# The product e(e+2) of Mish: from VectorE to GpSimd for four of the first five hidden tiles of a block

## The chip, the cores and the metric

The kernel runs on one core of a Trainium2 chip. A core has five engines, each of which works through a queue of its own in order: TensorE (PE in the profile; its weight loads are PEld), VectorE (DVE), ScalarE (ACT), GpSimd (POOL) and SyncE (SP, which issues the DMAs). Semaphores order them. The metric is the device time of one execution in microseconds (us).

## The reference

One transformer block with modulated layer norms, float32, one sequence of 2048 tokens, width 512, 32 heads of 16, hidden width 1792:

```
sa, ca, ga, sb, cb, gb = split(silu(c) @ w_mod)
h = layernorm(x) * (1 + ca) + sa
x = x + ga * (softmax(q k^T / 4) v @ wo)          # q, k, v = h @ wqkv
h = layernorm(x) * (1 + cb) + sb
x = x + gb * (mish(h @ w1 + b1) @ w2)             # mish(z) = z * tanh(log(1 + exp(z)))
```

With e = exp(z), tanh(log(1 + e)) = e(e+2) / (e(e+2) + 2). The kernel works with that form: u = e(e+2), r = exp(-log(u + 2)), one Newton step on r, and z * u * r.

## The kernel before

**Steps.** Attention is cut into 4 blocks of 512 queries (NB) and 8 groups of 4 heads (G), and each pair of these into 16 chunks of 128 keys, so that there are T = 512 steps t. A step makes four score products (`score`, L529, 128 keys by 512 queries), whose exponential ScalarE writes as `pr` (L532), and four products of 128 queries by 512 keys for the row maxima of a later group (`max_tile`, L480), which VectorE reduces to `mx` (L482). At its end stand the products of the exponentials with v, for the step two before (`pv`, L547). Scores and maxima go through one PSUM ring of 6 banks (`ring`): TensorE can write a bank only after ScalarE or VectorE has read the product that was in it.

**Half steps.** Time in the program is counted in half steps h = 2t and 2t + 1. `at(h, f)` puts a piece of work into the list of half step h. In `step`, `run_hooks(2 * t)` issues the first list ahead of the step's products, and `run_hooks(2 * t + 1)` issues the second in the midst of the products, at `i == len(mine) // 2`. An early-listed piece thus stands in its engine's queue ahead of the four exponentials or maxima of its step, and one of an odd half step stands between them: where a step's part of a unit has six slots, after the first exponential and after the second maximum.

**Units beside the attention.** The output projection and the dense layers of a query block that is done run beside the attention of the next ones. Their work is cut into units of 12 matmuls (24 of half the width in a block's first up unit), fed from a list, half of them in each pair of steps; one unit takes four steps. `block(qb, t0)` makes the list for each of the first three query blocks; the fourth is done by `tail()` after the last step. An up unit `up_unit(f)` computes hidden tile f, 128 of the 1792 hidden values (f = 0 to 13) for 512 tokens. The list begins with up units 0, 1, 2, 3, 4 one right after the other (so every 8 half steps one ends); then down units (back to width 512, `down_unit`) and up units take turns, so that an up unit ends every 16 half steps.

**Mish.** When an up unit's last matmul is issued, its `fin(h)` runs: it issues stage s1 and lists the other stages of `mish` at h plus a lag:

- s1 (L737, ScalarE): hb = product + bias, frees the PSUM bank `bk` that the next unit writes
- s2 (L740, ScalarE): ee = relu(10 - hb), with which e is capped
- s2b (L743, ScalarE): ee = exp(10 - ee), which is e
- s3 (L747 or L749 and L750): ee = e(e+2), on VectorE as one instruction if `own`, otherwise on GpSimd as two; then on GpSimd hb = hb * ee (L751) and qq = ee + 2 (L753)
- s4 (L756, ScalarE): rr = log(ee + 2)
- s5 (L759, ScalarE): rr = exp(-rr), then six instructions on GpSimd (L765 to L768, then `hi_copy` L95 and `lo_sub` L98), which leave the hidden tile as the pair a_h, a_l that the down units read

For f = 0, 1, 2 the lags are 2, 4, 5, 6, 8, so s5 falls together with s1 of the next up unit. For f = 3, whose result the first down units wait for, they are 1, 2, 3, 4, 6. For f = 4 and above they are taken from the free even half steps, s3 half a step after s2b, and s4 in the next even one, mostly 2, 4, 5, 6 and a later one for s5. `idle(h)` is true for half steps late in the third block's time, where no maxima are left and VectorE has room.

The profile's execution shows 42 such up units; 17 have the product on VectorE (5 in each of the three blocks, and 2 in idle half steps), 25 on GpSimd. The 14 hidden tiles of the tail have it on VectorE.

Of the kernel before, what the change touches and what calls it, by code (L numbers as in the profile page):

```python
# [18 lines left out]
def adaln_block(ctx: ExitStack, tc: tile.TileContext, x, wqkv, wo, w1, b1, w2, c, w_mod, out):  # L19
# [142 lines left out]
    def bank(tag="ms"):  # L162
        return ring() if tag == "ring" else ps.tile([P, TB], F32, tag=tag, name="bk", bufs=1)
# [38 lines left out]
    def at(h, f):  # L202

        hooks.setdefault(h, []).append(f)
# [508 lines left out]
    def up_mms(acc, w, hh, hl, parts=1):  # L713
        for c in range(parts):
            s = slice(c * TB // parts, (c + 1) * TB // parts)
            mm3(acc[:, s], [w1v(w, 0, k) for k in range(DK)], [w1v(w, 1, k) for k in range(DK)],
                [hh[:, k, s] for k in range(DK)], [hl[:, k, s] for k in range(DK)], "b")
# [58 lines left out]
    def idle(h):  # L776

        return h is not None and 2 * (T - PRO) + 2 < h <= 2 * T
# [6 lines left out]
    def block(qb, t0):  # L785
# [7 lines left out]
        def load(h, d, load_, keys):  # L793

            for j, k in enumerate(keys):
                at(h + 2 * j, lambda k=k: d.__setitem__(k, load_(k)))
# [76 lines left out]
        def up_unit(f, tag):  # L873
            mst["norming"] = False
            w = w1s.pop(f)
            acc = bank(tag)
            up_mms(acc, w, *hx, parts=1 if f else 2)
            stages = mish(f, acc, False, act)

            def fin(h):  # L880
                stages[0](idle(h))
                own = f < 5 or idle(h + 5)
                if f < 4:
                    lags = (1, 2, 3, 4, 6) if f == 3 else (2, 4, 5, 6, 8)
                else:

                    free = [i for i in range(2, 16, 2) if i != 8 and (h + i) % 32 != 4]
                    lags = (free[0], free[1], free[1] + 1, free[2], free[3])
                for i, s in zip(lags, stages[1:]):
                    at(h + i, (lambda s=s: s(True)) if i == lags[2] and own else s)  # L890
                done["a", f] = h + lags[-1]
                nxt = state[qb + (f + 2) // FT][1] if f + 2 < FT or qb < NB - 2 else None
                if nxt is None:
                    if f == FT - 1:
                        load(h + 1, state[last][1], w1_tail, (2, 3))
                else:
                    load(h, nxt, load_w1, ((f + 2) % FT,))
            return fin
# [58 lines left out]
        for gi in range(2):  # L957
            f = 4 * gi + 5
# [526 lines left out]
```

## Time and profile before

| | |
|---|---|
| median of 3 runs | 1699.01 us (1698.46 to 1699.34) |
| profiled execution, its own time | 1697.49 us |
| its span | 1695.7 us |
| TensorE busy | 99% |
| VectorE / ScalarE / GpSimd busy | 85% / 80% / 48% |
| mean granted TensorE clock | 0.999 of full speed |

How to read it: the span is that of the instructions in the trace, and the execution's own time has some 1.8 us more around it. The rows of the order of time show the start in us from the span's start, the duration, the engine, the line in the code, the operation, output and inputs, the count of merged instructions, and in brackets how long the engine sat idle before and what ended that. Neighbouring instructions on VectorE and ScalarE overlap a little, so that four exponentials of about 0.6 us each take 2.06 us. The rows with L547 mark the end of a step: the time from one to the next is the length of a step.

### The profile page before, as it was taken

To read this page: it belongs to the slowest core of one execution; us is meant where nothing else is said; L and a number is where in the kernel's file an instruction comes from. 1 tells how busy PE (TensorE), PEld (TensorE's weight loads), DVE (VectorE), ACT (ScalarE), POOL (GpSimd) and SP (SyncE) were. 2 spreads that over 40 slices of the span, in tenths; PEclk is the share of its full clock that TensorE was granted. 3 is DMA by queue.
4 is the path that set the end of the run, shared out by engine and by line. 5 is a ranking of instruction groups with operands and counts; after the bars stand their busy time and mean duration, and the time that the engine had idled before them with its cause. 6 is when DMAs were issued, how large, how long until landed. Compare 5 with 4: busy or idle time off the path is not lost.

```text
span 1695.7 us, 33728 instructions
## 1 busy us (share of the span) xinstructions
PE 1672.8 (99%) x12406; PEld 924.7 (55%) x12406; DVE 1437.8 (85%) x2370; ACT 1358.3 (80%) x2612; POOL 820.1 (48%) x838
## 2 busy tenths in 40 slices
PE   7999999999999999999999999999999999999999
PEld 5755665555445455555555455555555455555587
DVE  6888888888899888888889898888889988884378
ACT  6247777777778988888888998888888988888674
POOL 6456223665413464655423564555323564555442
PEclk9999999999999999999999999999999999999999
DMA  6887546777755342534355434434354433433261
GB/s 234 237 274 193 135 127 185 232 218 212 229 170 140 100 107 75 136 80 126 81 155 148 117 74 98 134 72 134 84 142 128 130 93 77 143 107 128 77 230 62
DMA packets 114029, 238.44 MB, mean 141 GB/s; under 512 B 23824, under 2 KB 49424, under 8 KB 107912
## 3 DMA queue, kind: packets, MB, share of 16 engines
q1 hardware_dynamic: 113864, 236.28, 49.3%
q8 instruction: 98, 1.61, 0.4%
q14 instruction: 67, 0.55, 0.1%
HBM read 179.95 MB, written 51.44 MB: 136 GB/s over the span
## 4 chain that ended last, share of the span: by engine, by line
PE 91%; DVE 4%; ACT 2%; DMA 2%; issue 0%; SPq 0%; POOL 0%; ACTq 0%; DVEq 0%
PE bk L547 29%; PE ring L529 23%; PE ring L480 20%; PE bk L136 9%; PE bk L129 3%; PE ring L1156 2%; DVE mx L482 2%; PE ring L129 2%; ACT pr L532 1%; DMA xt<-in_A_x 1%; PE ring L494 1%; DMA qa<-mt 1%; PE ring L859 0%; PE ring L509 0%; DVE hf L392 0%
## 5 line engine op out<-in xcount | busy, mean ns | idle before, releaser
L482 DVE TENSOR_REDUCE mx<-ring 128x1 f32<-128x512 f32 x1968 | 1223.0, 682 | 153.1 <-PE ring L480 137.4
L532 ACT ACTIVATE pr<-ring 128x512 f32<-128x512 f32 x2048 | 1078.3, 602 | 209.1 <-PE bk L136 121.1
L480 PE MATMUL ring<-ka,qa 64*128 64x512 f32 x1968 | 818.8, 430 | 1.6 <-ACT pr L532 1.1
L529 PE MATMUL ring<-qa,ka 64*128 64x512 f32 x2048 | 760.8, 403 | 5.4 <-DMA qa<-mt 2.6
L547 PE MATMUL bk<-pr,vg 128*32 128x512 f32 x4096 | 545.1, 604 | 0.0
L480 PEld LDWEIGHTS ring<-ka,qa 64*128 64x128 f32 x1968 | 351.2, 184 | 327.8 <-DVE mx L482 251.0
L529 PEld LDWEIGHTS ring<-qa,ka 64*128 64x128 f32 x2048 | 374.1, 184 | 199.0 <-DVE mx L482 114.7
L136 PE MATMUL bk<-h,w 64*128 64x512 f32 (+1 forms) x1080 | 278.9, 391 | 0.0
L136 PE MATMUL bk<-w,a_h 64*128 64x512 f32 x632 | 210.6, 413 | 0.0
L136 PEld LDWEIGHTS bk<-h,w 64*128 64x128 f32 x1080 | 178.3, 184 | 9.5 <-ACT pr L532 1.5
L547 PEld LDWEIGHTS bk<-pr,vg 128*32 128x32 f32 x4096 | 80.7, 108 | 136.2 <-issue 126.6
L136 PE MATMUL bk<-w,a_l 64*128 64x512 f32 x316 | 124.1, 393 | 0.0
L136 PEld LDWEIGHTS bk<-w,a_h 64*128 64x128 f32 x632 | 107.0, 184 | 2.2
L915 POOL TENSOR_TENSOR y<-yd,y 128x512 f32<-128x512 f32 x44 | 56.9, 1294 | 89.4 <-ACT yd L914 84.5
L749 POOL TENSOR_SCALAR qq<-ee 128x512 f32<-128x512 f32 x25 | 15.6, 624 | 169.3 <-ACT ee L743 169.3
L765 POOL TENSOR_TENSOR qq<-qq,rr 128x512 f32<-128x512 f32 x42 | 54.3, 1292 | 83.4 <-ACT rr L759 83.3
L751 POOL TENSOR_TENSOR hb<-hb,ee 128x512 f32<-128x512 f32 x42 | 54.2, 1291 | 82.3 <-DVE ee L747 80.4
L136 PE MATMUL bk<-w,o_hl 64*128 64x512 f32 x288 | 79.1, 405 | 0.0
L98 POOL TENSOR_TENSOR a_l<-hb,a_h 128x512 fp32r<-128x512 f32 x53 | 72.1, 1361 | 4.4
L136 PEld LDWEIGHTS bk<-w,a_l 64*128 64x128 f32 x316 | 58.3, 184 | 2.4
L136 PE MATMUL bk<-h_h,wl 64*128 64x512 f32 x168 | 57.7, 425 | 0.0
L95 POOL TENSOR_SCALAR qh<-qf 128x512 fp32r<-128x512 f32 x27 | 16.8, 622 | 82.8 <-ACT qf L259 56.3
(210 smaller groups left out, 1909.0 us busy)
## 6 DMA issues: line engine op xcount, KB each, us to landing
ka<-kscr SPq DMA_DIRECT2D x124, 384.0 KB
w<-w2scr SPq DMA_DIRECT2D x56, 512.0 KB
w<-w1scr SPq DMA_DIRECT2D x46, 512.0 KB
vg<-vscr SPq DMA_DIRECT2D x32, 552.0 KB
qa<-qscr SPq DMA_DIRECT2D x124, 100.0 KB
kscr<-qh SPq DMA_DIRECT2D x16, 512.0 KB
qscr<-qh SPq DMA_DIRECT2D x32, 256.0 KB
w2scr<-hl SPq DMA_DIRECT2D x14, 512.0 KB
```

Of the source, the lines that this page charges most:

```text
L98: (nc.gpsimd if eng == "p" else nc.vector).tensor_sub(lo, src, hi.bitcast(F32))
L129: nc.tensor.matmul(acc, l, r, start=start, stop=stop)
L136: i = nc.tensor.matmul(acc, l[64 * g:64 * g + 64], r[64 * g:64 * g + 64], start=start and not then, stop=bool(stop and then))
L480: nc.tensor.matmul(pm, qt[64 * s:64 * s + 64, qs * P:(qs + 1) * P], kt[64 * s:64 * s + 64, kb * TB:(kb + 1) * TB], start=True, stop=True)
L482: nc.vector.tensor_reduce(out=mxs[n][:, s, 4 * j + qs, kb:kb + 1], in_=pm, op=ALU.max, axis=AX.X)
L529: nc.tensor.matmul(p_, kt[64 * s:64 * s + 64, kc * P:(kc + 1) * P], qt[64 * s:64 * s + 64, :], start=True, stop=True)
L532: e = nc.scalar.activation(pr, p_, AF.Exp, scale=SCALE)
L547: nc.tensor.matmul(accs[n][32 * h:32 * h + 32, :], vgs[n][:, o:o + 32], pts.pop((t, h)), start=(kc == 0), stop=(kc == 15))
L751: (nc.vector if tail else nc.gpsimd).tensor_mul(hb, hb, ee)
L765: nc.gpsimd.tensor_mul(qq, qq, rr)
L915: nc.gpsimd.tensor_add(y[i], yd, y[i])
L1156: nc.tensor.matmul(po[i // 2][:, i % 2, :], l[:, s], w[:, r, :], start=(f == 0 and j == 0), stop=(f == FT - 1 and j == 2))
```

## The change

For hidden tiles 0, 1, 2 and 4 of each of the first three blocks, e(e+2) is no longer one instruction on VectorE but two on GpSimd, in the same half step (lag 5). For tiles 0, 1 and 2 the logarithm is listed half a step later (lag 7 and not 6). Tile 3 stays on VectorE with its own lags; tile 4 has its lags from the free even half steps as before. The lag of s5, and with it the time from which down units may be issued, is the same.

```diff
             def fin(h):
                 stages[0](idle(h))
-                own = f < 5 or idle(h + 5)
+                own = f == 3 or idle(h + 5)
                 if f < 4:
-                    lags = (1, 2, 3, 4, 6) if f == 3 else (2, 4, 5, 6, 8)
+                    lags = (1, 2, 3, 4, 6) if f == 3 else (2, 4, 5, 7, 8)
                 else:
 
                     free = [i for i in range(2, 16, 2) if i != 8 and (h + i) % 32 != 4]
                     lags = (free[0], free[1], free[1] + 1, free[2], free[3])
                 for i, s in zip(lags, stages[1:]):
                     at(h + i, (lambda s=s: s(True)) if i == lags[2] and own else s)
```

Stage s3, whose branch `own` chooses:

```python
        def s3(own=False):
            if tail or own:
                nc.vector.scalar_tensor_tensor(ee, ee, 2.0, ee, op0=ALU.add, op1=ALU.mult)
            else:
                nc.gpsimd.tensor_scalar(qq, ee, 1.0, 2.0, op0=ALU.mult, op1=ALU.add)
                nc.gpsimd.tensor_mul(ee, ee, qq)
            (nc.vector if tail else nc.gpsimd).tensor_mul(hb, hb, ee)
            if not tail:
                nc.gpsimd.tensor_scalar(qq, ee, 1.0, 2.0, op0=ALU.mult, op1=ALU.add)
```

## The prediction

> **What bounds the kernel now.** I read the page first, then the groups by line, then the order of time of one early hidden tile and of one late one.
>
> ```profile
> span 1695.7 us, 33728 instructions
> PE 1672.8 (99%) x12406; PEld 924.7 (55%) x12406; DVE 1437.8 (85%) x2370; ACT 1358.3 (80%) x2612; POOL 820.1 (48%) x838
> PE 91%; DVE 4%; ACT 2%; DMA 2%; issue 0%; SPq 0%; POOL 0%; ACTq 0%; DVEq 0%
> ```
>
> TensorE ends nearly everything: 91% of the chain that ended last, against 4% for VectorE. Relieving VectorE everywhere would find little to win. But shares are means, and the change acts in three short stretches. There, a late and an early tile differ. First tile 5 of the second block, with its product already on GpSimd: TensorE's step marks, then ScalarE.
>
> ```profile
> 1013.45 1.07 PE L547 MATMUL bk<-pr,vg 128*32 128x512 f32 x8
> 1016.29 1.06 PE L547 MATMUL bk<-pr,vg 128*32 128x512 f32 x8
> 1019.13 1.07 PE L547 MATMUL bk<-pr,vg 128*32 128x512 f32 x8
> ```
> ```profile
> 1014.31 0.73 ACT L756 ACTIVATE rr<-ee,two 128x512 f32<-128x512 f32 x1
> 1015.21 1.63 ACT L532 ACTIVATE pr<-ring 128x512 f32<-128x512 f32 x3 [0.16 <-PE bk L136]
> ```
>
> The step with the logarithm takes 2.84 us, and so does the next: TensorE's own pace. ScalarE runs the logarithm while TensorE is still busy with the products by v; the first exponential then waits 0.16 us for its score product, not for the logarithm. At the start of a step the logarithm is free. Now tile 1 of the second block.
>
> ```profile
> 954.44 1.06 PE L547 MATMUL bk<-pr,vg 128*32 128x512 f32 x8
> 957.27 1.06 PE L547 MATMUL bk<-pr,vg 128*32 128x512 f32 x8
> 959.96 0.50 PE L480 MATMUL ring<-ka,qa 64*128 64x512 f32 x1 [0.24 <-ACT pr L532]
> 960.62 1.07 PE L547 MATMUL bk<-pr,vg 128*32 128x512 f32 x8
> ```
> ```profile
> 955.28 0.75 ACT L756 ACTIVATE rr<-ee,two 128x512 f32<-128x512 f32 x1
> 956.20 1.63 ACT L532 ACTIVATE pr<-ring 128x512 f32<-128x512 f32 x3 [0.17 <-PE bk L136]
> 957.73 0.68 ACT L737 ACTIVATE hb<-bk,b1c 128x512 f32<-128x512 f32 x1
> 958.30 0.60 ACT L532 ACTIVATE pr<-ring 128x512 f32<-128x512 f32 x1
> 958.78 0.64 ACT L759 ACTIVATE rr<-rr 128x512 f32<-128x512 f32 x1
> 959.30 2.07 ACT L532 ACTIVATE pr<-ring 128x512 f32<-128x512 f32 x4
> ```
>
> The logarithm's step is again free (2.83 us). The next takes 3.35 us: the following tile's first stage (L737) and this tile's last exponential (L759) crowd into it. From 956.20 to 961.37 (959.30 + 2.07) ScalarE has no gap, and TensorE stops at 959.96 for an exponential. So in this stretch ScalarE is the bound, by 0.51 us per tile, and its only unused time lies before 956.20.
>
> **The product moves.** 12 products go over: tiles 0, 1, 2, 4 in three blocks.
>
> ```profile
> L747 DVE SCALAR_TENSOR_TENSOR ee<-ee 128x512 f32<-128x512 f32 x31 | 25.0, 806 | 15.0 <-ACT ee L743 15.0
> L749 POOL TENSOR_SCALAR qq<-ee 128x512 f32<-128x512 f32 x25 | 15.6, 624 | 169.3 <-ACT ee L743 169.3
> L750 POOL TENSOR_TENSOR ee<-ee,qq 128x512 f32<-128x512 f32 x25 | 32.1, 1285 | 2.1
> ```
>
> VectorE loses 12 x 0.81 = 9.7 us, nearly all of it hidden already, since the logarithm's step above was at 2.83 us with the product in it. The worst case I take is tile 2 of the first block:
>
> ```profile
> 586.38 1.06 PE L547 MATMUL bk<-pr,vg 128*32 128x512 f32 x8
> 589.54 1.06 PE L547 MATMUL bk<-pr,vg 128*32 128x512 f32 x8
> 592.63 0.64 PE L547 MATMUL bk<-pr,vg 128*32 128x512 f32 x4
> ```
>
> That step takes 3.16 us, but the next only 3.09, as ScalarE used the delay to catch up: 6.25 us for two against 2.83 + 3.35 = 6.18 above. The relief is 0.07 us there and mostly nothing elsewhere: **-0.1 us** in all, with 9 x 0.32 = 2.9 us as the limit if no step gave anything back.
>
> GpSimd gains 12 x 1.91 = 23 us. Behind the product on its queue stand hb * ee, qq and then the six instructions of s5:
>
> ```profile
> 952.75 1.29 POOL L98 TENSOR_TENSOR a_l<-hb,a_h 128x512 fp32r<-128x512 f32 x1
> 954.67 1.29 POOL L751 TENSOR_TENSOR hb<-hb,ee 128x512 f32<-128x512 f32 x1 [0.62 <-DVE ee L747]
> 955.92 0.63 POOL L753 TENSOR_SCALAR qq<-ee 128x512 f32<-128x512 f32 x1
> 959.56 1.28 POOL L765 TENSOR_TENSOR qq<-qq,rr 128x512 f32<-128x512 f32 x1 [3.02 <-ACT rr L759]
> ```
>
> GpSimd is free at 954.04, so e(e+2) is there at about 956.0 (0.62 + 1.29 and the small gaps between), qq at about 958.0, still ahead of the 959.56 at which s5 begins. The 3.02 us of idle time is the cover; if it went, hidden tiles would come later to the down units. No DMA and no SyncE work is moved, and s5 keeps its lag.
>
> **The logarithm of tiles 0, 1, 2 moves half a step.** It now stands behind the first exponential of its step. VectorE's product of lag 5 already stands in such a place, between maxima. ScalarE would have nothing from about 955.3 until the first score at 956.20, run one exponential (0.49) to 956.69, then the logarithm, then two exponentials, L737, one exponential, L759 and the four of the next step. All of that was gapless, so all of it shifts by what a logarithm takes of the queue:
>
> ```profile
> 1371.23 0.72 ACT L756 ACTIVATE rr<-ee,two 128x512 f32<-128x512 f32 x1 [0.48 <-DVE ee L747]
> 1371.85 1.86 ACT L532 ACTIVATE pr<-ring 128x512 f32<-128x512 f32 x3
> ```
>
> That is 0.62 us from start to start. TensorE's stop at 959.96 is released by the first of those four exponentials, so it comes 0.62 us later, and the step mark at 960.62 with it. The step of 3.35 us becomes about 3.97. Nothing later returns it, as TensorE's pace of 2.84 us is the floor. Nine tiles: 9 x 0.62 = **+5.6 us**. Bounds: 0, if the ring's six banks hid it, and 9 x 0.72 = 6.5 with the full duration. I take 0.62, as the row of a gapless queue is nearest.
>
> Does GpSimd make it in time? Above, 956.0 against 956.69: yes. In tile 2 of the first block, less so:
>
> ```profile
> 585.41 1.30 POOL L98 TENSOR_TENSOR a_l<-hb,a_h 128x512 fp32r<-128x512 f32 x1
> ```
>
> Free at 586.71, product at about 588.75; the logarithm's turn is 586.38 + 1.76 + 0.49 = 588.63 (the offset of the first exponential from the mark, 956.20 - 954.44). A wait of 0.1 us, twice or so: **+0.2 us**. Bounds: 0, and 9 x 0.48 = 4.3 us with the wait of the row above in each.
>
> **Tile 4 keeps its lags.** With GpSimd idle, its product is like tile 5's: no idle time ahead of the logarithm at 1014.31. So nothing in the first and second block. In the third, GpSimd is on the attention's normalization:
>
> ```profile
> 1369.30 1.28 POOL L98 TENSOR_TENSOR o_hl<-od,o_hl 128x512 fp32r<-128x512 f32 x1
> 1371.21 1.28 POOL L751 TENSOR_TENSOR hb<-hb,ee 128x512 f32<-128x512 f32 x1 [0.63 <-DVE ee L747]
> ```
>
> Free at 1370.58, product at about 1372.6; the logarithm, which ran at 1371.23 after 0.48 us of waiting, now waits to 1372.63, with the exponentials behind it and the ring behind those: **+1.4 us**. Bounds: 3 x 1.4 = 4.2 us, if GpSimd were as late in each of the three blocks, and -0.5, if the wait that is there vanished.
>
> Of the Trainium skill, "GPSIMD Engine Reference", section "Engine selection", puts elementwise work on VectorE, with GpSimd about twice as slow for two inputs. The rows agree on the duration (1.91 us against 0.81) but not on the consequence, since the tile 5 logarithm found its product ready; taken as a delay of 1.1 us in each tile 4, the rule would make 3.3 us of my 1.4.
>
> **The sum:** 5.6 + 0.2 + 1.4 - 0.1 = 7.1 us. The profiled execution took 1697.49 us, 1.52 below the median of the runs; it would become 1704.6, and the median 1706.1.
>
> **The rivals.** (1) The ring hides the later logarithm: 0.2 + 1.4 - 0.1 = +1.5 us, 1700.5. For it: at the start of a step it cost nothing. Against: the gapless queue, and TensorE's stop on an exponential in it. It decides if the steps of 3.35 us stay there.
>
> (2) Faster: VectorE's product is itself what stretches the pairs of steps. By the code every such pair has one in it, so this trace has no pair without it to compare. Then each pair falls from 6.18 to 2 x 2.84 = 5.68: 9 x 0.50 = 4.5 us, and with tile 4's wait of 0.48 gone too -5.0, 1694.0. It passes 0.2% from seven pairs on, and not at all if tile 4 loses its 1.4 us. It needs ScalarE to show gaps where it shows none. "Perfetto Trace Analysis" of the Trainium skill, section "Optimizing Scalar/DVE Operations", says that a saturated VectorE may be helped by offloading even to GpSimd, though the two share a read port; here VectorE isn't the saturated one in these steps.
>
> (3) GpSimd becomes the bound: each of the nine logarithms waits 0.48 us more, 1706.1 + 4.1 = 1710.2. Against it: 3.02 us of idle time per tile.
>
> **How the numbers follow.** A change within 0.2%, 3.4 us, is about what a measurement here can't tell from none. My forecast (1703 to 1708.5) has 0.68, rival 1 0.15, rival 2 0.09, rival 3 0.08. Slower 0.76, same 0.15, faster 0.09. Range 1700.3 to 1709.5: it takes in rival 1 and part of rival 3, and leaves out rival 2 and the top.
>
> **What would show it.** L749 runs 37 times and L747 19; VectorE's busy time falls by some 9 us. Nine steps of about 3.35 become about 3.97, with some 0.9 us of ScalarE idle ahead of the first exponential in the step before. The third block's tile 4 shows a wait of about 1.9 us for GpSimd. Wrong if those nine steps keep their length or shrink.

## The result, and the profile after

The changed kernel takes 1704.0 us in the median of 7 runs, against 1698.46 us of the kernel before (7 runs): 1.0034 of its time, 95% interval 1.0025 to 1.0043. It is slower by 5.5 us. The profiled execution took 1703.24 us, its span is 1701.5 us, 5.8 more than the span before.

The page of the changed kernel, and from its groups by line the product and the logarithm (columns: count, then busy time and mean duration in ns, then the idle time before them and its releaser):

```profile
span 1701.5 us, 33713 instructions
PE 1673.6 (98%) x12406; PEld 924.5 (54%) x12406; DVE 1435.4 (84%) x2358; ACT 1357.7 (80%) x2612; POOL 842.5 (50%) x862
```
```profile
L747 DVE SCALAR_TENSOR_TENSOR ee<-ee 128x512 f32<-128x512 f32 x19 | 15.2, 798 | 15.0 <-ACT ee L743 15.0
L749 POOL TENSOR_SCALAR qq<-ee 128x512 f32<-128x512 f32 x37 | 23.1, 623 | 224.6 <-ACT ee L743 224.6
L756 ACT ACTIVATE rr<-ee,two 128x512 f32<-128x512 f32 x56 | 40.5, 722 | 12.5 <-DVE ee L747 10.6 <-POOL ee L750 1.8
```

Twelve products moved: 31 to 19 on VectorE, 25 to 37 on GpSimd, which is 22 us busier. VectorE's product group is 9.8 us smaller, its whole busy time only 2.4 us; most of the gap is a single tiny instruction at the start of the kernel (L359) that this execution shows at 5.6 us (0.25 before), far from the change. GpSimd's product is named as what the logarithm waited for once, with 1.8 us.

The same tile 1 of the second block, in order of time, first TensorE's step marks and its one stop, then ScalarE:

```profile
956.38 1.06 PE L547 MATMUL bk<-pr,vg 128*32 128x512 f32 x8
959.23 1.06 PE L547 MATMUL bk<-pr,vg 128*32 128x512 f32 x8
962.45 0.49 PE L480 MATMUL ring<-ka,qa 64*128 64x512 f32 x1 [0.27 <-ACT pr L532]
963.11 1.06 PE L547 MATMUL bk<-pr,vg 128*32 128x512 f32 x8
```
```profile
958.14 0.60 ACT L532 ACTIVATE pr<-ring 128x512 f32<-128x512 f32 x1 [0.78 <-PE ring L529]
958.64 0.71 ACT L756 ACTIVATE rr<-ee,two 128x512 f32<-128x512 f32 x1
959.25 1.07 ACT L532 ACTIVATE pr<-ring 128x512 f32<-128x512 f32 x2
960.21 0.70 ACT L737 ACTIVATE hb<-bk,b1c 128x512 f32<-128x512 f32 x1
960.78 0.62 ACT L532 ACTIVATE pr<-ring 128x512 f32<-128x512 f32 x1
961.25 0.66 ACT L759 ACTIVATE rr<-rr 128x512 f32<-128x512 f32 x1
961.77 2.09 ACT L532 ACTIVATE pr<-ring 128x512 f32<-128x512 f32 x4
```

ScalarE now idles 0.78 us ahead of the step's first exponential; the logarithm, which had filled that time, stands behind it. From there on the queue is as full as before and half a microsecond later. The step with the logarithm takes 2.85 us (2.83 before), the next 3.88 (3.35). TensorE stops at the same place for the same exponential. In all nine tiles (0, 1, 2 of three blocks) the two steps together grew by 0.52 to 0.57 us, 5.0 us in sum.

Tile 4 of the third block, before (three step marks and TensorE's stop between the first two) and after (the same, then ScalarE):

```profile
1369.75 1.06 PE L547 MATMUL bk<-pr,vg 128*32 128x512 f32 x8
1371.79 0.49 PE L480 MATMUL ring<-ka,qa 64*128 64x512 f32 x1 [0.30 <-DVE mx L482]
1373.41 1.06 PE L547 MATMUL bk<-pr,vg 128*32 128x512 f32 x8
1376.24 1.06 PE L547 MATMUL bk<-pr,vg 128*32 128x512 f32 x8
```
```profile
1374.24 1.06 PE L547 MATMUL bk<-pr,vg 128*32 128x512 f32 x8
1378.30 0.49 PE L480 MATMUL ring<-ka,qa 64*128 64x512 f32 x1 [1.18 <-ACT pr L532]
1378.72 1.07 PE L547 MATMUL bk<-pr,vg 128*32 128x512 f32 x8
1381.66 0.64 PE L547 MATMUL bk<-pr,vg 128*32 128x512 f32 x4
```
```profile
1377.05 0.72 ACT L756 ACTIVATE rr<-ee,two 128x512 f32<-128x512 f32 x1 [1.82 <-POOL ee L750]
```

Its two steps went from 6.49 to 7.42 us, +0.93. Before, TensorE stopped there for VectorE's maxima; after, for ScalarE's exponentials. With the nine tiles that makes 5.9 us, against a difference of 5.8 us between the spans. In the first and second block tile 4's steps did not change (3.15 and 2.84 us after, 3.15 and 2.85 before).

### The profile page after: what moved, and what is told of

Same layout as the page of the kernel before. It is cut to its first block, busy times and chain, and to the rows that moved or that the text cites. A ratio compares the mean times of both kernels' runs of the same rounds, so it can differ in the third digit from the quotient of the medians.

```text
span 1701.5 us, 33713 instructions
## 1 busy us (share of the span) xinstructions
PE 1673.6 (98%) x12406; PEld 924.5 (54%) x12406; DVE 1435.4 (84%) x2358; ACT 1357.7 (80%) x2612; POOL 842.5 (50%) x862
## 4 chain that ended last, share of the span: by engine, by line
PE 87%; DVE 4%; ACT 3%; issue 2%; DMA 2%; POOL 2%; POOLq 0%; ACTq 0%; SPq 0%; DVEq 0%
PE bk L547 27%; PE ring L529 21%; PE ring L480 18%; PE bk L136 10%; PE bk L129 3%; PE ring L1156 2%; DVE mx L482 2%; PE ring L129 2%; ACT pr L532 2%; PE ring L494 1%; POOL ql L98 1%; DMA w2scr<-hl 0%; PE ring L859 0%; DMA kscr<-qh 0%; DMA hl<-in_B_w 0%
## 5 line engine op out<-in xcount | busy, mean ns | idle before, releaser
L749 POOL TENSOR_SCALAR qq<-ee 128x512 f32<-128x512 f32 x37 | 23.1, 623 | 224.6 <-ACT ee L743 224.6
L98 POOL TENSOR_TENSOR a_l<-hb,a_h 128x512 fp32r<-128x512 f32 x53 | 72.1, 1360 | 4.4
```

Source lines behind the costliest of these rows:

```text
L98: (nc.gpsimd if eng == "p" else nc.vector).tensor_sub(lo, src, hi.bitcast(F32))
```

## The experiments

Each experiment's time stands beside runs of the kernel before on the same chip. Where a term is under 1 us it is read from the steps, step by step against the trace before.

**The later logarithm alone.** The product stays on VectorE.

```diff
-                    lags = (1, 2, 3, 4, 6) if f == 3 else (2, 4, 5, 6, 8)
+                    lags = (1, 2, 3, 4, 6) if f == 3 else (2, 4, 5, 7, 8)
```

> The product stays on VectorE as before; only the logarithm of tiles 0, 1, 2 moves from lag 6 to lag 7. If the place of the logarithm in ScalarE's queue is what costs, the whole cost of the nine tiles is here: the steps with L737 and L759 go from 3.2-3.5 to about 3.9-4.1 us, 9 x 0.55 = +5.0 us, and tile 4 of the third block keeps its step of 3.66 us. If GpSimd is what costs (its two instructions, or the later hb * ee behind them), nothing happens: within 0.5 us of the kernel before.

Measured: 1703.99 us against 1699.39, ratio 1.0026 (1.0016 to 1.0035). The nine tiles cost 0.49 to 0.57 us each, 4.9 in sum; tile 4's step stays. The step marks and ScalarE at tile 1 of the second block:

```profile
958.22 1.07 PE L547 MATMUL bk<-pr,vg 128*32 128x512 f32 x8
961.06 1.07 PE L547 MATMUL bk<-pr,vg 128*32 128x512 f32 x8
964.95 1.06 PE L547 MATMUL bk<-pr,vg 128*32 128x512 f32 x8
```
```profile
959.98 0.60 ACT L532 ACTIVATE pr<-ring 128x512 f32<-128x512 f32 x1 [0.78 <-PE ring L529]
960.48 0.71 ACT L756 ACTIVATE rr<-ee,two 128x512 f32<-128x512 f32 x1
```

The same picture without any product moved: 0.78 us of idle time, then a step of 2.84 and one of 3.89 us. So the place of the logarithm in ScalarE's queue costs what the change costs at these tiles.

**The products alone.** All four go to GpSimd, the logarithm stays at lag 6.

```diff
-                own = f < 5 or idle(h + 5)
+                own = f == 3 or idle(h + 5)
```

> The products of tiles 0, 1, 2, 4 go to GpSimd, the logarithm stays at lag 6, at the start of its step. Tile 0: GpSimd is free, no wait, nothing lost. Tiles 1 and 2: GpSimd still finishes the tile before when their exponential is done, its product comes 0.5 to 1.3 us after the time at which the first exponential of the step could run, so ScalarE waits: by the queue theory six times about 1 us, with 0.9 us at tile 4 of the third block +6.9 us. If the later place alone is what costs and waits are absorbed by the ring, only the 0.9 us of tile 4 are left.

Measured: 1705.86 us against 1699.39, ratio 1.0039 (1.0026 to 1.0052). ScalarE waits for GpSimd's product in tiles 1 and 2 of every block, by 0.62 to 1.34 us, and by 1.84 at the third block's tile 4. The worst of the six, tile 1 of the third block:

```profile
1339.84 0.72 ACT L756 ACTIVATE rr<-ee,two 128x512 f32<-128x512 f32 x1 [1.34 <-POOL ee L750]
1340.47 1.55 ACT L532 ACTIVATE pr<-ring 128x512 f32<-128x512 f32 x3
```
```profile
1337.50 1.06 PE L547 MATMUL bk<-pr,vg 128*32 128x512 f32 x8
1341.52 1.06 PE L547 MATMUL bk<-pr,vg 128*32 128x512 f32 x8
```

That step takes 4.02 us; with the next, 1.1 us more than before. The six tiles lose 5.1 us, tile 4 loses 0.95. Tile 0 lost nothing in the first and second block, as expected, but its two steps in the third are 0.28 us longer, which I can't explain; the run with tile 0's product alone on GpSimd (below) does not show it. The ring doesn't absorb the waits. With the logarithm half a step later, the change avoids these waits and pays about as much for the place: 5.0 us for its nine tiles against 5.1 for these six.

**Tile 4's product alone.**

```diff
-                own = f < 5 or idle(h + 5)
+                own = f < 4 or idle(h + 5)
```

> Only tile 4's product goes to GpSimd, its lags are the same as before. By the trace of the changed kernel: nothing in the first and second block, one step of about 4.5 us instead of 3.66 in the third, 0.9 us in all (within what the times can tell, so it is read from the steps). If GpSimd's longer instructions cost by themselves, each of the three tiles shows a longer step by about 1 us.

Measured: 1699.94 us against 1699.39, ratio 1.0002 (0.9993 to 1.0011), no difference by the times. The steps show +0.95 us at the third block's tile 4 and nothing at the two others:

```profile
1372.67 0.72 ACT L756 ACTIVATE rr<-ee,two 128x512 f32<-128x512 f32 x1 [1.84 <-POOL ee L750]
```
```profile
1369.85 1.06 PE L547 MATMUL bk<-pr,vg 128*32 128x512 f32 x8
1374.36 1.06 PE L547 MATMUL bk<-pr,vg 128*32 128x512 f32 x8
```

GpSimd's 1.91 us are no loss where GpSimd is free. Where it is not, the wait is the one in the changed kernel.

**The change without tile 4.**

```diff
-                own = f < 5 or idle(h + 5)
+                own = f in (3, 4) or idle(h + 5)
```

with lag 7 for the logarithm.

> The change without tile 4: products of tiles 0, 1, 2 on GpSimd, their logarithm at lag 7, tile 4 as before. If the parts add up, this is the changed kernel less 0.9 us: +5.0 us against the kernel before, and the same step lengths as with the later logarithm alone, to 0.1 us each, as VectorE's relief is worth nothing there.

Measured: 1704.88 us against 1699.39, ratio 1.0034 (1.0022 to 1.0046). By the steps the nine tiles cost 5.0 us, as with the later logarithm alone (4.9). So taking the nine products off VectorE is worth nothing, to 0.1 us in sum. The single steps do get shorter (tile 2 of the first block 3.16 to 2.84 us), and the next step is longer by that much more.

**Tile 0's product alone, logarithm at lag 6.**

```diff
-                own = f < 5 or idle(h + 5)
+                own = 0 < f < 5 or idle(h + 5)
```

> Only tile 0's product goes to GpSimd, its logarithm stays at lag 6. GpSimd is idle there for some 19 us before the first block's tile 0, so the product is ready in time: no step changes by more than 0.1 us. If GpSimd's product is too slow for lag 6 in itself (1.91 us against 0.68), each of the three tiles shows a wait ahead of its logarithm.

Measured: 1698.5 us against 1699.32, ratio 0.9996 (0.9987 to 1.0004). No step of the three tiles changes by 0.1 us, although VectorE no longer has the product there: this tests rival 2 without a moved logarithm, and the pairs stay long (6.39, 6.17 and 6.44 us, against 6.40, 6.17 and 6.42 before). A product on a free GpSimd is neither a gain nor a loss.

**The first stage of tiles 1, 2, 3 on VectorE.** This takes L737 out of the crowded steps of the kernel before; nothing else is changed.

```diff
-                stages[0](idle(h))
+                stages[0](0 < f < 4 or idle(h))
```

> The kernel before, with the first stage (product + bias) of tiles 1, 2, 3 on VectorE in place of ScalarE, so that the crowded step holds only the exponential of the tile before. If ScalarE's queue is the bound of those nine steps, they fall from 3.1-3.5 to about 2.85-3.0 us: -4.5 us, less what VectorE's 0.6 us more in that step costs (four maxima take 2.48 us of 2.84, so up to 0.25 us each): -2 to -4.5 us. If VectorE's product is what stretches the pairs, a further instruction on VectorE makes them longer: +2 us or more.

Measured: 1696.33 us against 1699.32, ratio 0.9984 (0.9976 to 0.9993). Tile 1 of the second block, ScalarE, the new instruction on VectorE, and the step marks:

```profile
956.18 2.12 ACT L532 ACTIVATE pr<-ring 128x512 f32<-128x512 f32 x4 [0.17 <-PE bk L136]
958.19 0.63 ACT L759 ACTIVATE rr<-rr 128x512 f32<-128x512 f32 x1
958.79 2.08 ACT L532 ACTIVATE pr<-ring 128x512 f32<-128x512 f32 x4
960.77 0.71 ACT L740 ACTIVATE ee<-hb,hcap 128x512 f32<-128x512 f32 x1
```
```profile
957.75 0.74 DVE L735 TENSOR_SCALAR hb<-bk,b1c 128x512 f32<-128x512 f32 x1
```
```profile
954.42 1.07 PE L547 MATMUL bk<-pr,vg 128*32 128x512 f32 x8
957.26 1.06 PE L547 MATMUL bk<-pr,vg 128*32 128x512 f32 x8
960.17 1.07 PE L547 MATMUL bk<-pr,vg 128*32 128x512 f32 x8
```

The crowded step falls from 3.35 to 2.91 us, with more work on VectorE and the product still there. From tile 0's logarithm to tile 3's, the steps of the three blocks gain 3.4 us in sum; three single steps elsewhere, longer by 0.26 to 0.29 us without a cause that I can name, take back some of it in the profiled execution. So it was ScalarE that stretched these steps, not VectorE's product.

**The same in the changed kernel** (products on GpSimd, logarithm at lag 7, first stage of tiles 1, 2, 3 on VectorE).

> The changed kernel (products on GpSimd, later logarithm) with the first stage of tiles 1, 2, 3 on VectorE. ScalarE's queue then holds the logarithm in the place of L737: the nine steps should be back at about 3.35 us, and the whole at the kernel before plus the 0.9 us of tile 4: +0.5 to +1.5 us. If the late logarithm costs for another reason than the queue behind it, the +5 us stay.

Measured: 1700.06 us against 1699.32, ratio 1.0005 (0.9997 to 1.0014). The nine tiles' steps are back where they were in the kernel before: the pairs differ by at most 0.05 us each. What is left is tile 4's 0.93 us. The crowded step of tile 1 in the second block:

```profile
959.25 1.07 PE L547 MATMUL bk<-pr,vg 128*32 128x512 f32 x8
962.56 1.07 PE L547 MATMUL bk<-pr,vg 128*32 128x512 f32 x8
```

It takes 3.31 us, against 3.88 in the changed kernel and 3.35 in the kernel before. The later logarithm thus costs through the queue behind it: take one instruction of its size out of that queue, and the step is back at its old length. The cost is made up for and not abolished: with the first stage moved and everything else as before, the same step takes 2.91 us.

**The last exponential one step later**, in the kernel before.

```diff
-                    lags = (1, 2, 3, 4, 6) if f == 3 else (2, 4, 5, 6, 8)
+                    lags = (1, 2, 3, 4, 6) if f == 3 else (2, 4, 5, 6, 10)
```

> The kernel before, with the last exponential of tiles 0, 1, 2 one step later (lag 10 and not 8), at the start of the step that holds the next tile's L740. By the queue theory the step with L737 falls from 3.35 to 2.85 us, and the step with two instructions at its start goes from 2.84 to about 3.15: 9 x -0.2 = -1.8 us. If only the count of ScalarE's instructions in these four steps counts, nothing changes.

Measured: 1698.21 us against 1699.32, ratio 0.9993 (0.9985 to 1.0002): a small gain or none. The crowded step does fall to 2.83 to 2.86 us where nothing else is in it, and the next one grows by 0.22 to 0.23 us behind tile 2 and where the attention's evacuation is in the crowded step, and not at all elsewhere. But the tiles are ready later. VectorE's product now meets GpSimd's work and takes 1.1 us in tiles 1 and 2, and in each block a down unit waits for GpSimd, by 0.64, 0.38 and 0.20 us. The first block (step marks, and the matmul that waited):

```profile
609.47 1.06 PE L547 MATMUL bk<-pr,vg 128*32 128x512 f32 x8
612.58 0.49 PE L136 MATMUL bk<-w,a_l 64*128 64x512 f32 x1 [0.64 <-POOL a_l L98]
613.24 1.06 PE L547 MATMUL bk<-pr,vg 128*32 128x512 f32 x8
```

That step takes 3.77 us in place of 2.84. My estimate of 1.8 us left out who reads the later result.

**The normalization four half steps later**, in the changed kernel. In the third block GpSimd is on it when tile 4's product comes.

```diff
-            at(2 * t1 + (33 if g == 1 and qb < NB - 1 else 29 if g == 1 else 16 if hurry else 23), norm)
+            at(2 * t1 + (33 if g == 1 else 16 if hurry else 23), norm)
```

> The changed kernel, with the normalization (L590, L95, L98 on GpSimd) that stands ahead of the third block's tile 4 four half steps later, as it is in the first two blocks. If the place of GpSimd's normalization is what makes tile 4's logarithm wait, its step of 4.48 us falls to about 2.85: 1.6 us less than the changed kernel, about +4.3 us against the kernel before. If GpSimd is late there for its own backlog of tile 3, the wait stays.

Measured: 1704.39 us against 1699.85, ratio 1.0023 (1.0014 to 1.0032). Tile 4 of the third block:

```profile
1377.29 0.73 ACT L756 ACTIVATE rr<-ee,two 128x512 f32<-128x512 f32 x1
```
```profile
1376.42 1.07 PE L547 MATMUL bk<-pr,vg 128*32 128x512 f32 x8
1379.26 1.06 PE L547 MATMUL bk<-pr,vg 128*32 128x512 f32 x8
```

No wait, and a step of 2.84 in place of 4.48 us. The normalization ahead of the product was the cause.

**Both repairs in the kernel before**: first stage of tiles 1, 2, 3 on VectorE, and the later normalization; all products and lags as they were.

```diff
-            at(2 * t1 + (33 if g == 1 and qb < NB - 1 else 29 if g == 1 else 16 if hurry else 23), norm)
+            at(2 * t1 + (33 if g == 1 else 16 if hurry else 23), norm)
 ...
-                stages[0](idle(h))
+                stages[0](0 < f < 4 or idle(h))
```

> The kernel before with the first stage of tiles 1, 2, 3 on VectorE and the same later normalization. Tile 4's product on VectorE then meets no GpSimd work: its step of the third block falls from 3.66 to about 2.85 us, 0.8 us less than with the first stage alone: -3 us against the kernel before, the fastest of all. If VectorE's slow product there (1.49 us) has another cause, nothing is added to the -2.3 us.

Measured: 1694.72 us against 1699.85, ratio 0.9969 (0.9957 to 0.9981), the fastest of all. That is 5.1 us, more than the 3 expected, and the interval begins at 3.2; the steps of the stretches concerned account for 4.1 us (3.4 with tiles 0 to 3, 0.66 with tile 4), and I can't name the rest. Tile 4 of the third block: VectorE's product in the kernel before, then in this one, then this one's step marks.

```profile
1369.65 1.49 DVE L747 SCALAR_TENSOR_TENSOR ee<-ee 128x512 f32<-128x512 f32 x1
```
```profile
1368.00 0.68 DVE L747 SCALAR_TENSOR_TENSOR ee<-ee 128x512 f32<-128x512 f32 x1
```
```profile
1368.10 1.07 PE L547 MATMUL bk<-pr,vg 128*32 128x512 f32 x8
1370.96 1.06 PE L547 MATMUL bk<-pr,vg 128*32 128x512 f32 x8
```

The product is back at 0.68 us and the step at 2.86 in place of 3.66. With the first stage alone moved, the product there still takes 1.47 us and the step 3.64, so it is the normalization that made the difference.

## Why the prediction was right, point by point

**The direction and the mechanism** held. 7.1 us were forecast and 5.5 measured, within the stated range; the working was somewhat too pessimistic in three of its four terms. The range alone would prove little, since it also took in rival 1 (1700.5 us); it is the steps that tell the two apart.

**The later logarithm: forecast +5.6, measured +5.0** (4.9 alone). The mechanism is shown twice: alone it makes the cost, and with L737 taken out of the queue behind it the steps are back at their old length. The size was off by 0.07 us per tile, since the queue wasn't quite gapless, although the prediction read it so. Before, the three exponentials ahead of L737 took 1.53 us from the start of the first to L737 (956.20 to 957.73), 0.51 each; after, the two behind the logarithm took 0.96 (959.25 to 960.21), 0.48 each. Gaps of some hundredths of a microsecond, too small to be marked in the rows, gave back 0.08 of the 0.62 us.

**Waits for GpSimd in tiles 1 and 2: forecast +0.2, measured 0.** No logarithm of the nine tiles shows a wait. In tile 2 of the first block and tile 1 of the third it came 2.29 us after the step's mark, 0.03 to 0.04 later than in most of the others, so the estimate of 0.1 was right to within the gaps; the margin was as thin as it looked. Without the later place the waits are real, 0.62 to 1.34 us.

**Tile 4: forecast +1.4, measured +0.93.** The wait came as forecast (1.82 us; 1.9 was worked out), and the first and second block stayed free. The mis-sized step is that I took the difference of ScalarE's two waits, 1.82 - 0.48, for the difference of the steps. The step before was 0.82 us too long with a wait of only 0.48, because VectorE's slow product also held back the maxima, as TensorE's stop at 1371.79, ended by VectorE, shows. That loss went away with the move, and should have been set against the new one.

**VectorE's relief: forecast -0.1, measured 0** (4.9 with the products on VectorE, 5.0 without). The argument that what one step loses to the product comes back in the next was right.

**The rivals.** The ring didn't hide the later logarithm: the steps went from 3.35 to 3.88 us. VectorE's product wasn't what stretched the pairs: they stay long without it (tile 0's product alone), and get short when ScalarE is relieved instead. GpSimd wasn't the bound in tiles 1 and 2 with the later logarithm, though it would have been with the old one. A delay in each tile 4, because GpSimd is the slower engine for such work, is not what this case shows: only the third block's has it. A late product costs only where GpSimd is busy with something else.

## What to carry to other kernels

In a queue that is worked in order, the price of an instruction depends on where it stands against the other engine's phases: the same logarithm cost nothing at the start of a step, while TensorE was busy with the products by v, and 0.55 us one exponential later. Before an instruction is moved to a freer engine, look at which engine is crowded in that stretch, by the order of time and not by the page's shares; here the busier engine on the page (VectorE, 85%) had room in the crowded steps and ScalarE (80%) had none, and moving nine instructions off ScalarE won what moving twelve off VectorE could not. When a wait is moved, compare steps of the bounding engine, not waits of the one that waits.

## What was not expected of the hardware

VectorE's product of one tile takes 0.68 us when GpSimd is idle, and up to 1.49 us beside GpSimd's work in the kernel before; with GpSimd's normalization moved away, the very same instruction went from 1.49 to 0.68 us. Of the fifteen products of the three blocks before, the five that meet no GpSimd instruction take 0.68 us. The other ten start while a GpSimd instruction with two inputs is running, and each ends 0.54 to 0.56 us after that instruction's end, whatever its own duration (0.73 to 1.49 us). Two of them; the GpSimd instructions beside them are the rows of L98 at 952.75 and 585.41 in the prediction, which end at 954.04 and 586.71:

```profile
953.86 0.73 DVE L747 SCALAR_TENSOR_TENSOR ee<-ee 128x512 f32<-128x512 f32 x1
586.29 0.97 DVE L747 SCALAR_TENSOR_TENSOR ee<-ee 128x512 f32<-128x512 f32 x1
```

Of the Trainium skill, "SBUF — State Buffer", section "SBUF: two separate sides", says that VectorE, for an instruction with two SBUF inputs, and GpSimd lock a shared port against each other for a whole instruction. That agrees with these numbers; no run here shows the lock itself.
